# Weighted sums of V move wholly off the matrix engine in eleven of sixteen head groups of a two-layer decode step

## The chip, the cores and the metric

One core of a Trainium2 chip runs the kernel. The metric is the device time of one execution in microseconds (us). The kernel before took 676.72 us (median of 3 runs, 676.02 to 676.72).

## What is computed

A decode step for one token passes twice through an attention block and an MLP block, with the same weights and the same caches both times:

```python
def _A_ref(x, k_cache, v_cache, wq, wo):              # D=512, H=32 heads, Sk=4096 keys, Dh=128
    q = (x @ wq).reshape(B, Sq, H, Dh)                # heads to the front
    scores = jnp.einsum("bhqd,bhkd->bhqk", q, k_cache) * (Dh ** -0.5)
    p = _softmax(scores, axis=-1)
    o = jnp.einsum("bhqk,bhkd->bhqd", p, v_cache)
    return o.reshape(B, Sq, H * Dh) @ wo
def _B_ref(x, w1, b1, w2, b2):                        # F=1376
    return _gelu(x @ w1 + b1) @ w2 + b2
...
x = x + _A_ref(_layernorm(x), ...)
x = x + _B_ref(_layernorm(x), ...)
x = x + _A_ref(_layernorm(x), ...)
x = x + _B_ref(_layernorm(x), ...)
```

All is float32. The caches K and V hold 32 x 4096 x 128 elements each (64 MiB), and each is read once per layer.

## The kernel before, in words

**Groups.** The 32 heads are cut into G = 8 groups of J = 4. A layer runs n = 0 to 7 over the groups (layer 1 in the reverse order of heads, so that it begins with what still lies on the chip). A group's K is 128 x 16384 elements (8 chunks of NC = 2048 columns), its V the same, and one transfer of 128 x 4096 brings two weights: wo for this group and wq for the next.

**What a group does.** `queries` makes the group's queries z: four VectorE (DVE) operations over wq, a TensorE (PE) sum over the partitions, then DVE again. `scores` multiplies z with the 8 chunks of K on PE: 32 matmuls, which the trace shows as 64 passes, into the PSUM tile pS. `softmax` reads pS on DVE, takes the exponential on ScalarE (ACT), transposes on PE, and leaves the weights in pt. Then V is weighted and summed over the keys. `scaled_out` takes this sum from the PSUM tile pO and divides by the softmax's sum, and `head_out` multiplies with wo and adds into one row in the PSUM tile pB.

**Two ways to weight V.** Without `vec` (the groups n = 6 and 7 of layer 0 and all of layer 1), `values` does it on PE: 4 matmuls for each chunk with pt as the small operand. With `vec` (layer 0, n = 0 to 5) six of the eight chunks are multiplied in place, four by DVE (L268) and two by ACT (L265, 32 small operations), DVE adds the six into one chunk (L276, L278), and PE sums this one over its partitions with ones (`add_weighted`, L282) behind the two chunks that it still weights itself (L254). There, `add_weighted`, `scaled_out` and `head_out` of group n are called `late`, after the scores of group n+1 in the program; the program leaves their place on the engines to the framework's scheduler, save for what `pin` and `load` fix in the written order.

**Transfers.** All transfers go through one queue in program order, issued by SyncE (SP, L88). One large SBUF tile, `arena`, is cut by hand into homes. Layer 0 rotates three homes of 8 chunks through K and V. In layer 1, K has one home (columns 8 to 16 NC) and V one (0 to 8 NC). `PAIR` is the single home of the two weights. A transfer waits until all readers of its home are done, and all later transfers wait behind it.

**The end.** In the last group (n = 7, `final`) K comes in two halves and V in pieces, with small matmuls (`idle`, L420) between them; then wo, the MLP's w2 in four pieces, the MLP (`mlp`, its second product at L395), one addition (L598) and the store.

Of the kernel before, what the change touches and what calls it, by code (L numbers as in the profile page):

```python
# [17 lines left out]
P = 128  # L18
# [26 lines left out]
W2_AT = tuple(SPARE + U * (c % 8) for c in range(FB)), tuple(2 * BLOCK + 2 * NC + U * c for c in range(FB))  # L45
# [12 lines left out]
VECTOR, SCALAR = 6, 2  # L58
# [3 lines left out]
def decode_layers(ctx: ExitStack, tc: tile.TileContext, k, v, w, w1, w2, out):  # L62
# [45 lines left out]
    def free_now(layer, n):  # L108

        if layer == 0:  # L110
            at = HELD + 2 * NC
        elif n == 0:
            at = 6 * NC
            return arena[:, at : at + U], arena[:, 11 * NC : 11 * NC + 4 * 129]
        else:
            at = 9 * NC if n == 1 else 2 * BLOCK + NC
# [90 lines left out]
    def queries(n, xc, wt, at, t=None, short=False):  # L207
        t = wt[:, 0, :] if t is None else t
        pin(nc.vector.tensor_scalar(t, wt[:, 0, :], xc[:, 0:1], None, op0=ALU.mult))
        for c in range(1, 4):  # L210
            nc.vector.scalar_tensor_tensor(t, wt[:, c, :], xc[:, c : c + 1], t, op0=ALU.mult, op1=ALU.add)  # L211
        if short:
            nc.tensor.matmul(at, one.to_broadcast([P, P]), t, start=True, stop=True)  # L213
            own = t.rearrange("p (j d) -> p j d", j=J)
            nc.vector.tensor_tensor(own, at.rearrange("p (j d) -> p j d", j=J),
                                    ident[:, None, :].to_broadcast([P, J, P]), op=ALU.mult)
            nc.vector.tensor_reduce(zq[:, :, C - 1], own, axis=AX.X, op=ALU.add)
# [6 lines left out]
    def scores(z, c, kt):  # L224
        for j in range(J):
            nc.tensor.matmul(pS[32 * j : 32 * j + C, :], z[:, j, C - 1 - c : 2 * C - 1 - c],  # L226
                             kt[:, j, :], start=(c == 0), stop=(c == C - 1))

    def softmax(sc, nsc, p):
        nc.vector.tensor_reduce(mx[:, 0:1], pS, axis=AX.X, op=ALU.max)  # L230
# [26 lines left out]
    def weighted(pt, at, a, b):  # L257

        own = arena[:, at + NC * a : at + NC * b].rearrange("p (r j d) -> p r j d", j=J, d=DH)
        for i in range(a, b):  # L260
            t = own[:, 4 * (i - a) : 4 * (i - a + 1)]
            if i >= vec - SCALAR:
                for r in range(4):
                    for j in range(J):
                        nc.scalar.activation(t[:, r, j], t[:, r, j], AF.Copy, scale=pt[:, j, i, r : r + 1])  # L265
                continue
            weight = pt[:, :, i, :].rearrange("p j b -> p b j")[:, :, :, None].to_broadcast([P, 4, J, DH])
            nc.vector.tensor_tensor(t, t, weight, op=ALU.mult)  # L268

    def sum_weighted(at, n):  # L270

        def part_of(a, b):
            return arena[:, at + NC * a : at + NC * b]

        half = n // 2
        nc.vector.tensor_tensor(part_of(0, half), part_of(0, half), part_of(half, n), op=ALU.add)  # L276
        for c in range(1, half):
            nc.vector.tensor_tensor(part_of(0, 1), part_of(0, 1), part_of(c, c + 1), op=ALU.add)  # L278

    def add_weighted(at):  # L280
        for j in range(J):
            nc.tensor.matmul(pO[32 * j : 32 * j + 4, :], one.to_broadcast([P, 4]),  # L282
                             by_head(chunk(arena[:, at : at + NC]))[:, j], start=False, stop=True)
# [22 lines left out]

    def head_out(on, wt, n):
        if layer == 0 and n < G - 1:
            t = wt[:, 0, :]
            nc.vector.tensor_scalar(t, t, on[:, 0:1], None, op0=ALU.mult)  # L310
            for d in range(1, 4):
                nc.vector.scalar_tensor_tensor(t, wt[:, d, :], on[:, d : d + 1], t, op0=ALU.mult, op1=ALU.add)  # L312
            nc.tensor.matmul(pB[0:1, :], one, t, start=n == 0, stop=n == G - 2)  # L313
# [332 lines left out]
```

## Time and profile before

| what | value |
|---|---|
| median of 3 runs | 676.72 us |
| time of the profiled execution | 676.74 us |
| its span, first to last instruction | 674.8 us |
| mean granted TensorE clock | 0.767 of full |
| moved by DMA | 285.31 MB, mean 423 GB/s |
| busy: PE / DVE / ACT | 364.0 / 259.1 / 84.1 us |

A page of the profile lists busy time by engine, a picture of the span in 40 slices, the chain of waits followed back from the last instruction, and groups of instructions by line with the mean duration of one. A timeline gives single instructions with their start from the span's beginning and what ended the idle time before them. PE matmuls in float32 appear as two passes each.

### The profile page before, as it was taken

What the parts mean: (1) busy time and instruction counts of PE and PEld (TensorE: products, weight loads), DVE (VectorE), ACT (ScalarE), POOL (GpSimd) and SP (SyncE); (2) the same over time, 40 slices, a digit from 0 to 9 for tenths busy, and PEclk for the clock granted to TensorE, in tenths of its full rate; (3) what the DMA queues carried; (4) which work ended last, traced back from release to release, by engine and by line L of the source; (5) the groups of instructions that cost most, each with busy time, mean ns of one, the idle gap of its engine ahead of it and who ended that gap; (6) DMA issues with size and microseconds to landing.
All of it is one profiled execution on the core that took longest, in us unless ns stands there. A gap on an engine that the chain in (4) does not pass through costs nothing.

```text
span 674.8 us, 6333 instructions
## 1 busy us (share of the span) xinstructions
PE 364.0 (54%) x2664; PEld 94.1 (14%) x2664; DVE 259.1 (38%) x446; ACT 84.1 (12%) x249; POOL 5.0 (1%) x24
## 2 busy tenths in 40 slices
PE   1521622616426146175887987473355544755596
PEld 1100100101001001011124321111011111111123
DVE  3059379295693964933322322120121011201212
ACT  0041060140500503202011200000000000000010
POOL 1000000000000000000000000000000000000000
PEclk9965766856757668578699999786797677866989
DMA  9999999999999999999999999999999999999995
GB/s 375 435 435 437 435 436 431 418 454 431 432 435 409 455 435 432 435 432 414 428 415 385 404 422 447 421 443 427 435 432 435 436 435 405 451 432 414 431 415 236
DMA packets 10979, 285.31 MB, mean 423 GB/s; under 512 B 1220, under 2 KB 1224, under 8 KB 3400
## 3 DMA queue, kind: packets, MB, share of 16 engines
q1 hardware_dynamic: 10952, 284.92, 98.7%
q8 instruction: 20, 0.33, 0.2%
q14 instruction: 7, 0.06, 0.0%
HBM read 284.92 MB, written 0.00 MB: 422 GB/s over the span
## 4 chain that ended last, share of the span: by engine, by line
DMA 58%; PE 23%; DVE 17%; issue 1%; another core or an unknown queue 0%; ACT 0%; DVEq 0%; SPq 0%; ACTq 0%
DMA arena<-in_k 26%; DMA arena<-in_v 26%; PE pS L226 13%; DMA arena<-in_w 6%; DVE arena L268 5%; DVE arena L276 4%; DVE arena L278 3%; PE pO L254 2%; DVE arena L312 1%; PE pS L420 1%; DVE arena L211 1%; PE pO L282 1%; PE pB L313 1%; PE pB L317 1%; PE pO L395 1%
## 5 line engine op out<-in xcount | busy, mean ns | idle before, releaser
L226 PE MATMUL pS<-arena,smalls 128*8 128x512 f32 x1024 | 148.8, 709 | 57.6 <-DMA arena<-in_k 55.6
L254 PE MATMUL pO<-arena,pt 128*4 128x512 f32 x720 | 107.5, 737 | 55.5 <-DMA arena<-in_v 55.1
L230 DVE TENSOR_REDUCE smalls<-pS 128x1 f32<-128x512 f32 x16 | 11.1, 692 | 199.3 <-PE pS L226 199.3
L236 ACT ACTIVATE arena<-pS,smalls 128x512 f32<-128x512 f32 x16 | 12.4, 777 | 457.1 <-DVE smalls L235 457.1
L213 PE MATMUL pS<-arena,smalls 128*128 128x512 f32 x12 | 12.5, 1141 | 98.6 <-DVE arena L211 98.6
L286 DVE STREAM_TRANSPOSE arena<-pO 128x512 f32<-128x512 f32 x16 | 11.5, 717 | 128.2 <-PE pO L254 124.7
L268 DVE TENSOR_TENSOR arena<-arena,pt 128x2048 f32<-128x2048 f32 x24 | 53.9, 2287 | 15.1 <-DMA arena<-in_v 15.1
L265 ACT ACTIVATE arena<-arena,pt 128x128 f32<-128x128 f32 x192 | 56.7, 386 | 22.0 <-DMA arena<-in_v 22.0
L226 PEld LDWEIGHTS pS<-arena,smalls 128*8 128x8 f32 x1024 | 30.2, 99 | 161.4 <-issue 137.8
L276 DVE TENSOR_TENSOR arena<-arena 128x6144 f32<-128x6144 f32 x6 | 39.3, 6553 | 0.0
L254 PEld LDWEIGHTS pO<-arena,pt 128*4 128x4 f32 x720 | 20.3, 97 | 125.9 <-issue 121.5
L211 DVE SCALAR_TENSOR_TENSOR arena<-arena,smalls 128x512 f32<-128x512 f32 x45 | 33.8, 750 | 0.9
L238 PE MATMUL pO<-ident,arena 128*128 128x128 f32 x64 | 11.4, 305 | 38.0 <-ACT arena L236 37.6
L317 PE MATMUL pB<-arena,smalls 128*1 128x512 f32 x56 | 25.2, 592 | 10.3 <-DVE smalls L291 6.6
L313 PE MATMUL pB<-arena,smalls 128*1 128x512 f32 x14 | 13.1, 1035 | 29.4 <-DVE arena L312 29.4
L278 DVE TENSOR_TENSOR arena<-arena 128x2048 f32<-128x2048 f32 x12 | 27.4, 2288 | 0.0
L213 PEld LDWEIGHTS pS<-arena,smalls 128*128 128x128 f32 x12 | 3.0, 311 | 108.9 <-DVE arena L211 108.9
L312 DVE SCALAR_TENSOR_TENSOR arena<-arena,smalls 128x512 f32<-128x512 f32 x21 | 15.8, 752 | 0.7
L238 PEld LDWEIGHTS pO<-ident,arena 128*128 128x128 f32 x64 | 7.3, 150 | 51.9 <-ACT arena L236 46.5
L420 PE MATMUL pS<-arena,ident 128*8 128x512 f32 (+1 forms) x34 | 14.2, 517 | 0.5 <-DVE pt L354 0.5
L420 PE MATMUL pO<-arena,ident 128*8 128x512 f32 (+1 forms) x30 | 11.6, 507 | 0.3 <-DVE smalls L189 0.3
L282 PE MATMUL pO<-arena,smalls 128*4 128x512 f32 x48 | 11.0, 1006 | 0.8
(114 smaller groups left out, 164.7 us busy)
## 6 DMA issues: line engine op xcount, KB each, us to landing
arena<-in_w SPq DMA_DIRECT2D x14, 2048.0 KB, 22.4
arena<-in_k SPq DMA_DIRECT2D x6, 4096.0 KB, 27.6
arena<-in_v SPq DMA_DIRECT2D x2, 4096.0 KB, 35.4
arena<-in_k SPq DMA_DIRECT2D x3, 2048.0 KB, 13.6
arena<-in_v SPq DMA_DIRECT2D x2, 2048.0 KB, 38.5
arena<-in_w SPq DMA_DIRECT2D x4, 1024.0 KB, 15.0
arena<-in_v SPq DMA_DIRECT2D x3, 1024.0 KB, 46.7
arena<-in_w SPq DMA_DIRECT2D x6, 512.0 KB, 12.2
```

The lines of the kernel that those rows point to most:

```text
L211: nc.vector.scalar_tensor_tensor(t, wt[:, c, :], xc[:, c : c + 1], t, op0=ALU.mult, op1=ALU.add)
L226: nc.tensor.matmul(pS[32 * j : 32 * j + C, :], z[:, j, C - 1 - c : 2 * C - 1 - c], kt[:, j, :], start=(c == 0), stop=(c == C - 1))
L238: nc.tensor.transpose(pT[:, b].rearrange("p j r -> p (j r)"), p[:, P * b : P * (b + 1)], ident)
L254: nc.tensor.matmul(pO[32 * j : 32 * j + 4, :], pt[:, j, c, :], by_head(vt)[:, j], start=(i == 0), stop=(i == of - 1))
L265: nc.scalar.activation(t[:, r, j], t[:, r, j], AF.Copy, scale=pt[:, j, i, r : r + 1])
L268: nc.vector.tensor_tensor(t, t, weight, op=ALU.mult)
L276: nc.vector.tensor_tensor(part_of(0, half), part_of(0, half), part_of(half, n), op=ALU.add)
L278: nc.vector.tensor_tensor(part_of(0, 1), part_of(0, 1), part_of(c, c + 1), op=ALU.add)
L312: nc.vector.scalar_tensor_tensor(t, wt[:, d, :], on[:, d : d + 1], t, op0=ALU.mult, op1=ALU.add)
L313: nc.tensor.matmul(pB[0:1, :], one, t, start=n == 0, stop=n == G - 2)
L317: nc.tensor.matmul(pB[0:1, :], on[:, d : d + 1], wt[:, d, :], start=n == 0 and d == 0, stop=n == G - 2 and d == 3)
L420: pin(nc.tensor.matmul(at[:C, :n], ident[:, :C], t[:, 0, :n], start=True, stop=True))
```

## The change

1. **Layer 0, n = 0 to 5.** All eight chunks of V are weighted off PE: chunks 0 to 3 by DVE (`weighted`), 4 to 7 by ACT (`weighted_by_act`, 64 operations in place of 32). DVE adds in pairs of chunks (`add_pair`, 128 x 4096 elements), three times, and then the last two chunks together.
2. **Layer 1, n = 2 to 6.** The same way is taken where before PE weighted all chunks. In n = 6, the last but one group, PE weights one pair (chunks 2 and 3), DVE four chunks and ACT two. The order of the pairs is given by `PAIRS`.
3. **Place of the late work.** `late` is now two parts. `late_sum` (ones products on PE, `scaled_out`, and wo's four DVE operations into `ot`, a home of its own) stands after chunk 4 of the next group's scores, and after chunk 3 in the final group; `late_out` (one PE product into pB) stands after the scores. These and their neighbours are pinned to the written order.
4. **wo by DVE in layer 1, too.** For n = 1 to 6 of layer 1 `head_out`'s four products on PE become four DVE operations and one product; the queries take the short way there as well. For n = 6 the copy of pB and `row_to_quadrants` come with `late_out`, in the midst of the final group.
5. **Homes.** In layer 1, from n = 2, V alternates between 0 to 8 NC and 6 to 14 NC, K lies from 15 NC (from n = 3) and the softmax's tiles at 14 NC. W2's second home and `ends` move to the low columns.

The core of the diff:

```diff
+        def add_pair(at, to, by):
+            a, b = (arena[:, at + NC * c : at + NC * (c + 2)] for c in (to, by))
+            pin(nc.vector.tensor_tensor(a, a, b, op=ALU.add))
+        def sum_over_keys(t, start):
+            for j in range(J):
+                pin(nc.tensor.matmul(pO[32 * j : 32 * j + 4, :], one.to_broadcast([P, 4]), by_head(t)[:, j],
+                                     start=start, stop=True))
...
             for c, t in tiles:
                 scores(z, c, t)
+                if late is not None and c == (3 if final else 4):
+                    late[0]()
             if late is not None:
-                late()
+                late[1]()
                 late = None
...
-            if vec:
-                weighted(pt, v_home, vec - SCALAR, vec)
-                weighted(pt, v_home, 0, 2)
+            if pairs:
+                first_pair = pairs[0]
+                last = layer == 1 and n == G - 2
+                for c in pairs[2 : 3 if last else 4]:
+                    for i in (0, 1):
+                        weighted_by_act(pt, here["v", g, c + i], c + i)
+                for c in pairs[:2]:
+                    for i in (0, 1):
+                        weighted(pt, here["v", g, c + i], c + i)
+                add_pair(v_home, *pairs[:2])
...
+            if pairs:
+                z = queries(n + 1, xc_l, wq_next, pS, short=True,
+                            between=lambda: add_pair(v_home, first_pair, pairs[2]))
+                if not last:
+                    add_pair(v_home, first_pair, pairs[3])
+                total, other = here["v", g, first_pair], here["v", g, first_pair + 1]
+                pin(nc.vector.tensor_tensor(total, total, other, op=ALU.add))
+                def late_sum(rl=rl, ot=ot, wt=wo_t, total=total, last=last):
+                    sum_over_keys(total, not last)
+                    summed_wo(scaled_out(rl, ot), wt, ot[:, :U])
+                def late_out(ot=ot, n=n):
+                    add_out(ot[:, :U], n)
+                    if n == G - 2:
+                        row = arena[:, PAIR : PAIR + U]
+                        nc.vector.tensor_copy(row, pB)
+                        row_to_quadrants(row)
```

**PE in a group of layer 0.** Before, from one group's softmax transposes (L238) to the next group's (L254: its own two chunks of V; L213: queries; L282: ones; L313: wo's row; L226: scores):

```order
L238 MATMUL pO<-ident,arena 128x128 x4
L254 MATMUL pO<-arena,pt 4x512 x8
L213 MATMUL pS<-arena,smalls 128x512
L282 MATMUL pO<-arena,smalls 4x512 x4
L313 MATMUL pB<-arena,smalls 1x512
L226 MATMUL pS<-arena,smalls 8x512 x32
```

Of the change, the same stretch (scores are L228, ones L277, wo's row L309):

```order
L240 MATMUL pO<-ident,arena 128x128 x4
L213 MATMUL pS<-arena,smalls 128x512
L228 MATMUL pS<-arena,smalls 8x512 x20
L277 MATMUL pO<-arena,smalls 4x512 x4
L228 MATMUL pS<-arena,smalls 8x512 x12
L309 MATMUL pB<-arena,smalls 1x512
```

The eight matmuls over V are gone, and the ones and wo's row no longer stand ahead of the scores.

**DVE in the same group**, from the weighting of V to the queries' last step. Before (L268 weighting, L276 and L278 sums, L209 to L217 queries):

```order
L268 TENSOR_TENSOR arena<-arena,pt 128x2048 x3
L209 TENSOR_SCALAR arena<-arena,smalls 128x512
L268 TENSOR_TENSOR arena<-arena,pt 128x2048
L211 SCALAR_TENSOR_TENSOR arena<-arena,smalls 128x512
L276 TENSOR_TENSOR arena<-arena 128x6144
L211 SCALAR_TENSOR_TENSOR arena<-arena,smalls 128x512
L278 TENSOR_TENSOR arena<-arena 128x2048
L211 SCALAR_TENSOR_TENSOR arena<-arena,smalls 128x512
L278 TENSOR_TENSOR arena<-arena 128x2048
L215 TENSOR_TENSOR arena<-pS,ident 128x512
L217 TENSOR_REDUCE smalls<-arena 128x4
```

Of the change (L273 is `add_pair`, L217 and L219 the queries' last two steps, L557 the sum's last addition):

```order
L268 TENSOR_TENSOR arena<-arena,pt 128x2048 x4
L273 TENSOR_TENSOR arena<-arena 128x4096
L209 TENSOR_SCALAR arena<-arena,smalls 128x512
L211 SCALAR_TENSOR_TENSOR arena<-arena,smalls 128x512 x3
L273 TENSOR_TENSOR arena<-arena 128x4096
L217 TENSOR_TENSOR arena<-pS,ident 128x512
L219 TENSOR_REDUCE smalls<-arena 128x4
L273 TENSOR_TENSOR arena<-arena 128x4096
L557 TENSOR_TENSOR arena<-arena 128x2048
```

Two pair additions now stand ahead of the queries' end, and the rest of the sum behind it. In layer 1 the groups n = 2 to 6 have this same list (n = 6 with one L273 less at the end).

**PE from the last but one group into the final one.** Before (L254 values, L317 wo's four products, L220 queries, L326 the row to its quadrants, L226 the final scores, L420 small matmuls):

```order
L254 MATMUL pO<-arena,pt 4x512 x32
L317 MATMUL pB<-arena,smalls 1x512 x4
L220 MATMUL pO<-smalls,arena 128x1 x4
L326 MATMUL pB<-arena,ident 1x128 x4
L226 MATMUL pS<-arena,smalls 8x512 x32
L420 MATMUL pO<-arena,ident 8x512 x3
L238 MATMUL pO<-ident,arena 128x128 x4
```

Of the change:

```order
L256 MATMUL pO<-arena,pt 4x512 x8
L213 MATMUL pS<-arena,smalls 128x512
L228 MATMUL pS<-arena,smalls 8x512 x16
L277 MATMUL pO<-arena,smalls 4x512 x4
L228 MATMUL pS<-arena,smalls 8x512 x16
L309 MATMUL pB<-arena,smalls 1x512
L326 MATMUL pB<-arena,ident 1x128 x4
L420 MATMUL pO<-arena,ident 8x512 x3
L240 MATMUL pO<-ident,arena 128x128 x4
```

The ones products, wo's row and its quadrants now stand between the final scores and the softmax's transposes. On DVE, the copy of pB stands ahead of the softmax's first reduction there:

```order
L303 TENSOR_SCALAR arena<-arena,smalls 128x512
L305 SCALAR_TENSOR_TENSOR arena<-arena,smalls 128x512 x3
L567 COPY arena<-pB 128x512
L232 TENSOR_REDUCE smalls<-pS 128x1
L234 STREAM_TRANSPOSE smalls<-smalls 128x32
```

Before, that copy (L562) stood ahead of the final scores and their reduction (L230) behind them with nothing of group n = 6 between.

More of the change, by code (lines that the diff above doesn't have):

```diff
@@ L304, in scaled_out_last, with summed_wo, add_out @@
         return on
-    def head_out(on, wt, n):
[L308 to L313, printed above, removed]
+    def summed_wo(on, wt, t):
+        pin(nc.vector.tensor_scalar(t, wt[:, 0, :], on[:, 0:1], None, op0=ALU.mult))
+        for d in range(1, 4):
+            pin(nc.vector.scalar_tensor_tensor(t, wt[:, d, :], on[:, d : d + 1], t, op0=ALU.mult, op1=ALU.add))
+        return t
+    def add_out(t, n):
+        pin(nc.tensor.matmul(pB[0:1, :], one, t, start=n == 0, stop=n == G - 2))
+    def head_out(on, wt, n):
+        if n < G - 1 and (layer == 0 or n > 0):
+            add_out(summed_wo(on, wt, wt[:, 0, :]), n)
             return
@@ L573, in decode_layers @@
         else:
[L575 removed]
+            ends = arena[:, 5 * NC : 5 * NC + 3 * P]
             xb = of_32(ends, 4)
```

90 lines of the change are left out of this document (38 added, 52 removed).

## The prediction

> **What bounds the kernel now.** I read the page first: busy time, the slices, then the chain of waits.
>
> ```profile
> PE 364.0 (54%) x2664; PEld 94.1 (14%) x2664; DVE 259.1 (38%) x446; ACT 84.1 (12%) x249; POOL 5.0 (1%) x24
> DMA  9999999999999999999999999999999999999995
> DMA 58%; PE 23%; DVE 17%; issue 1%; another core or an unknown queue 0%; ACT 0%; DVEq 0%; SPq 0%; ACTq 0%
> ```
>
> No engine is busy for more than 54%, and the transfers never pause until the last slice. The bytes stay as they are. So the change can move the time in two ways only: it lets the queue run dry, or it changes what stands behind the last transfers. First, the queue. The timeline of one group in layer 0, DVE and SP:
>
> ```profile
> 89.62 6.70 DVE L268 TENSOR_TENSOR arena<-arena,pt 128x2048 f32<-128x2048 f32 x3 [3.27 <-DMA arena<-in_v]
> 99.49 6.55 DVE L276 TENSOR_TENSOR arena<-arena 128x6144 f32<-128x6144 f32 x1
> 113.78 0.72 DVE L286 STREAM_TRANSPOSE arena<-pO 128x512 f32<-128x512 f32 x1 [0.63 <-PE pO L282]
> 115.54 2.33 DVE L312 SCALAR_TENSOR_TENSOR arena<-arena,smalls 128x512 f32<-128x512 f32 x3
> 119.81 0.33 SPq L88 DMA_DIRECT2D arena<-in_w  x1
> 127.35 0.69 DVE L230 TENSOR_REDUCE smalls<-pS 128x1 f32<-128x512 f32 x1 [9.48 <-PE pS L226]
> 133.25 2.29 DVE L268 TENSOR_TENSOR arena<-arena,pt 128x2048 f32<-128x2048 f32 x1 [2.11 <-DMA arena<-in_v]
> ```
>
> V lands at 89.6 and the next V at 133.25: 43.6 us for 18 units of 1 MiB (w 2, K 8, V 8), 433 GB/s. The next weights are issued at 119.81, 13.4 us before the transfer ahead of them is in. The queue has that much in reserve. Layer 1, where PE weights V alone, keeps the same pace by the chain, from one K's landing to the next:
>
> ```profile
> 518.65 34.55 DMA arena<-in_k
> 562.64 34.18 DMA arena<-in_k
> ```
>
> They end at 553.20 and 596.82, again 43.6 us apart. Layer 0's DVE and ACT work costs the transfers nothing, and PE's work in layer 1 neither: what is freed there was not waited for.
>
> Now the end, from the chain and PE's timeline:
>
> ```profile
> 606.64 33.89 DMA arena<-in_k
> 640.57 6.61 PE pS L226 x32
> 665.26 0.46 PE pS L343 x16
> 668.78 1.89 issue
> 670.67 1.10 PE pO L395 x32
> ```
>
> From the last half of K (640.53) on, the chain is compute: PE and DVE one behind the other, 28.3 us to 668.78. Then PE stands still for 1.89 us for nothing that the chain can name. The end is thus PE's and DVE's path, and the transfers are some 1 to 2 us ahead of it.
>
> **The change part by part.** *The queue in layer 0 and from n = 2 in layer 1.* I count from V's landing. Four weightings take 4 x 2.23 (6.70 / 3) = 8.9 us. A pair addition of 4096 elements stands between two rows: 6.55 us above and the 2.20 us of L278 below, so 4.4. The queries and their last steps:
>
> ```profile
> 106.71 2.20 DVE arena L278
> 625.96 0.48 DVE L209 TENSOR_SCALAR arena<-arena,smalls 128x512 f32<-128x512 f32 x1
> 626.48 2.33 DVE L211 SCALAR_TENSOR_TENSOR arena<-arena,smalls 128x512 f32<-128x512 f32 x3
> 111.74 0.69 DVE L215 TENSOR_TENSOR arena<-pS,ident 128x512 f32<-128x512 f32 x1
> 112.47 0.69 DVE L217 TENSOR_REDUCE smalls<-arena 128x4 f32<-128x512 f32 x1
> L265 ACT ACTIVATE arena<-arena,pt 128x128 f32<-128x128 f32 x192 | 56.7, 386 | 22.0 <-DMA arena<-in_v 22.0
> ```
>
> 2.85 and 1.42 us. Queries are ready at 8.9 + 4.4 + 2.85 + 4.4 + 1.4 = 22.0 us, the whole sum 4.4 + 2.2 later, at 28.5. ACT's 64 operations take 64 x 56.7 / 192 = 18.9 us, and the last pair is wanted at 22.0: hidden by 3 us. K lands 10 units after V, at 24.2. So queries wait for K, not K for queries. Twenty matmuls of scores come to 30.8 (their pace is below), the ones to about 32, then DVE's 4.1 us (113.78 to 117.87): the weights' home is free at about 36.3, not 30.2 as before (119.81 - 89.62). The reserve falls from 13.4 to 7.3 us but stays. SP's next two issues, K and V, stand behind it and come with it. The softmax begins at 36.3 (before: 127.35, so 37.7) and ends some 4 us later, ahead of V at 43.6. In layer 1 the terms are the same. Its next V waits for the first pair addition only, 13.3 us after V, and K is under way until 24.2: 10.9 us in reserve. All of this is off the path: nothing saved, nothing lost. Without the reserve each late microsecond would count eleven times.
>
> *n = 1 of layer 1.* Four DVE operations in place of PE's products add about 3 us ahead of the queries, which puts the scores of n = 2 at 424 instead of 421.26. The V that they are to weight lands at 440.7: covered.
>
> ```profile
> 421.26 7.05 PE L226 MATMUL pS<-arena,smalls 128*8 128x512 f32 x64 [0.26 <-DVE smalls L221]
> 440.72 9.22 PE L254 MATMUL pO<-arena,pt 128*4 128x512 f32 x64 [8.96 <-DMA arena<-in_v]
> ```
>
> *The final group.* Here K's first half came early, and before the queries were ready just in time for it:
>
> ```profile
> 616.30 8.48 PE L254 MATMUL pO<-arena,pt 128*4 128x512 f32 x64 [5.86 <-DMA arena<-in_v]
> 630.94 3.62 PE L226 MATMUL pS<-arena,smalls 128*8 128x512 f32 x32
> 640.57 6.56 PE L226 MATMUL pS<-arena,smalls 128*8 128x512 f32 x32 [6.01 <-DMA arena<-in_k]
> 629.74 0.69 DVE L562 COPY arena<-pB 128x512 f32<-128x512 f32 x1 [0.94 <-PE pB L317]
> 630.62 0.40 PE L326 MATMUL pB<-arena,ident 128*1 128x128 f32 x8
> 646.96 2.74 PE L420 MATMUL pO<-arena,ident 128*8 128x512 f32 x6
> 649.87 0.66 PE L238 MATMUL pO<-ident,arena 128*128 128x128 f32 x4 [0.18 <-ACT arena L236]
> ...
> 111.83 1.93 PE pO L282 x8
> 466.00 8.54 PE L226 MATMUL pS<-arena,smalls 128*8 128x512 f32 x64 [10.16 <-DMA arena<-in_k]
> 495.78 3.59 PE L317 MATMUL pB<-arena,smalls 128*1 128x512 f32 x8 [1.32 <-DVE smalls L291]
> 647.21 0.69 DVE L230 TENSOR_REDUCE smalls<-pS 128x1 f32<-128x512 f32 x1 [16.32 <-PE pS L226]
> 596.96 9.61 PE L226 MATMUL pS<-arena,smalls 128*8 128x512 f32 x64 [8.56 <-DMA arena<-in_k]
> ```
>
> V of n = 6 is there at 616.3. By the count above the final queries come at 616.3 + 22.0 = 638.3, where before the scores began at 630.94. The two halves of the scores then run one behind the other. The same 32 passes took 3.62 us at full clock and 6.56 after an idle stretch at half clock. PE will have idled, but the clock rises on the way: 64 passes in layer 1 took 8.54 to 9.61 us, so 1.3 to 2.4 us over twice 3.62. I take 5.7 for the first half (bounds 3.6 and 6.6): 644.0. The ones are 8 passes: 1.93 us in layer 0 (L282, at half clock), 0.9 at the scores' full-clock pace; PE has by then worked for 5.7 us, so I take 0.9: 644.9. Then two strands. PE runs the second half, 3.6 us. DVE runs transposes and wo's sum, 4.1 us, to 649.0. DVE is the later. L309 is one matmul, two passes. By the row of L317, eight passes in 3.59 us, it takes 0.9: 649.9. The copy of pB, 0.73 us with its wait: 650.65. Only now does the softmax's reduction start, which before began at 647.21. PE does L326, 0.4, and the three small matmuls, 2.6 (2.74 less the tail of the last): 653.7. DVE and ACT would be ready at 650.65 + 2.66 (647.21 to 649.87) = 653.3. So the transposes begin at 653.7 to 653.9 instead of 649.87: **3.9 us late**, bounds 1.8 (PE warm throughout) and 4.8 to 5.8 (cold throughout, the ones at 1.9).
>
> On the clock the Trainium skill ("TensorE: Matmul & The Clock Gate", Part 1) says that about 3.4 us of sustained work bring the full rate, in free-running windows. By it the first half would take an estimated 5.1 us and the total would be 0.6 us lower; the rows agree in kind (1.3 to 2.4 us lost at 0.092 us a pass is half clock for 2.9 to 5.3 us), and their middle is my 5.7.
>
> Behind the transposes the chain has no wait for data, so the 3.9 us travel down to 668.78. There the 1.89 us of standstill come in.
>
> ```profile
> 668.78:670.67 1.89, 0.00 (x0) 0.00 (x0) 0.00 (x0) 0.00 (x0) 0.00 (x0) 1.00 0.05 17
> q8 instruction: 20, 0.33, 0.2%
> q8 instruction: 1, 0.02, 2.7%
> ```
>
> The data were nearly in (DMA busy 5%), and the second row of instruction fetches is that of 667.5 to 670: one of the page's twenty lies just there. PE has 2664 weight loads and as many matmuls, 266 for each fetch of 16 KB: I read the standstill as PE waiting for code. The change takes 216 float32 matmuls off PE (864 such records, 3.4 fetches), so the boundary moves 0.4 of a fetch along and no longer stands here. It falls some 110 passes before the end, about 5 us of work after the boundary ahead of it. That is nearly the time from one boundary (128 passes earlier, in L343 at about 665.3) to the arrival here at 670.67, so I leave 0.2 us.
>
> The Trainium skill ("Runtime: NRT & Kernel Launch", Instruction fetch mechanics) has fetches of 256 instructions, mostly hidden. The size agrees with the twenty fetches; "hidden" does not agree with the 1.89 us. Were it right and the wait another one, 3.9 us of lateness would swallow that wait just as well: 0.2 us less.
>
> *Sum* against the profiled execution (676.74 us, span 674.8): +3.9 late, -1.89 standstill, +0.2 left = **+2.2 us: 678.9 us**. The median of the runs shown, 676.72, is the same time.
>
> **The rivals.** *The standstill's room takes it in* (no change). If PE is warm in the first half, or the adds or ones are a little shorter, the transposes come 1.8 us late: 676.74 + 1.8 - 1.89 + 0.2 = 676.8. For it: clock windows of all kinds occur here (7.05 us for 64 passes in one group). Against: PE has only one matmul in the 10 us or more ahead of the final scores.
>
> *The standstill comes back*: the new boundary costs what the old one did, in the MLP instead: 676.74 + 3.9 = 680.6. For it, the short margin above.
>
> *The queue runs dry.* If the late strand of a group is longer than 43.6 us from V to V, every such group pays. It decides from 7.3 us over my count; 1 us beyond that is 11 us in all, 688. Against: every term but the 4096-wide addition has its row.
>
> *Faster*, by one mechanism, the pair additions: two of them stand on the final queries' path. Should a 4096-wide one take 2.2 us like a 2048-wide, the queries are there at 633.9, the first half is over before K's second half lands, that half runs warm from 640.6, and the transposes begin at about 649.4: 0.4 us early. The standstill goes: 676.74 - 0.4 - 1.9 = 674.4, or some 675 where the last data bound it. It decides from about 2.6 us for an addition. Against it: 6.55 and 2.20 us for 6144 and 2048 elements are the same 1.07 ns for each.
>
> **How the numbers follow.** My forecast 0.50, no change 0.32, standstill back 0.06, queue dry 0.04, faster 0.08. A measurement here tells about 0.2% (1.35 us) from no change. Slower: 0.50 + 0.06 + 0.04 = 0.60; same 0.32; faster 0.08. The forecast's own range goes from 678.1 to 680.4. With no change taken in, and the standstill back, it is 675.9 to 681.4; the dry queue and most of faster lie outside.
>
> **What would show it.** Steps right: V to V still 43.6 us in both layers; weights issued 6 to 9 us before the transfer ahead lands; the final scores beginning at 638 and the transposes near 653.8; no standstill before the last matmuls. Wrong: an addition (L273) far from 4.4 us, a DMA slice below 9 in the middle, transposes before 652, or a PE standstill between 663 and the end.

## The result: slower by 0.56%, in two places

The changed kernel took 680.45 us (median of 6, 679.99 to 681.44), the kernel before, in the same comparison, 676.54 us (median of 6): a ratio of 1.0056 [1.0046, 1.0067]. In a second comparison it was 680.65 against 677.09 us, again 1.0056 [1.0044, 1.0069]. That is 3.6 to 3.9 us slower; forecast were 2.2 us (678.9) in a range from 675.9 to 681.4.

The profiled execution took 680.01 us, its span 678.2 us, 3.4 more than before. From its page (busy time; the slices of the transfers; the chain of waits):

```profile
PE 299.0 (44%) x2232; PEld 79.2 (12%) x2232; DVE 427.1 (63%) x521; ACT 224.8 (33%) x729; POOL 5.0 (1%) x24
DMA  9999999999999999999999999999999999999994
DMA 21%; DVE 12%; PE 6%; issue 0%; SPq 0%; DVEq 0%
```

PE gave up 65 us, DVE took on 168 us and ACT 141 us, and the transfers still have no pause that a slice of 17 us would show. A group of layer 0, timeline of DVE and of SP:

```profile
89.51 8.90 DVE L268 TENSOR_TENSOR arena<-arena,pt 128x2048 f32<-128x2048 f32 x4 [4.22 <-DMA arena<-in_v]
98.44 4.42 DVE L273 TENSOR_TENSOR arena<-arena 128x4096 f32<-128x4096 f32 x1
...
126.01 0.33 SPq L88 DMA_DIRECT2D arena<-in_w  x1
...
133.12 8.90 DVE L268 TENSOR_TENSOR arena<-arena,pt 128x2048 f32<-128x2048 f32 x4 [3.49 <-DMA arena<-in_v]
```

From V to V it is still 43.6 us. The next weights are issued 7.1 us before the transfer ahead of them is in (13.4 before). All that DVE and ACT do more there costs nothing.

The end, timeline of DVE and PE:

```profile
617.47 8.90 DVE L268 TENSOR_TENSOR arena<-arena,pt 128x2048 f32<-128x2048 f32 x4 [3.33 <-DMA arena<-in_v]
639.29 6.35 PE L228 MATMUL pS<-arena,smalls 128*8 128x512 f32 x32 [3.58 <-DVE smalls L219]
645.47 1.03 PE L277 MATMUL pO<-arena,smalls 128*4 128x512 f32 x8
646.33 3.61 PE L228 MATMUL pS<-arena,smalls 128*8 128x512 f32 x32
646.58 0.72 DVE L281 STREAM_TRANSPOSE arena<-pO 128x512 f32<-128x512 f32 x1 [5.14 <-PE pO L277]
650.72 1.02 PE L309 MATMUL pB<-arena,smalls 128*1 128x512 f32 x2 [0.78 <-DVE arena L305]
651.77 0.69 DVE L567 COPY arena<-pB 128x512 f32<-128x512 f32 x1 [1.11 <-PE pB L309]
652.38 0.68 DVE L232 TENSOR_REDUCE smalls<-pS 128x1 f32<-128x512 f32 x1
655.40 0.66 PE L240 MATMUL pO<-ident,arena 128*128 128x128 f32 x4
672.54 2.58 PE L395 MATMUL pO<-arena,smalls 128*1 128x128 f32 x88
```

V of n = 6 lands at 617.5 (I count from PE's first pass over it, 617.51) and the softmax's transposes begin at 655.40; before, these were 616.30 and 649.87. The last product (L395) now runs in one piece, without the standstill. So the 3.4 us of the span are these: V of n = 6 comes **1.2 us later**, the transposes come 37.89 us after it instead of 33.57 (**4.32 later**), the standstill of 1.89 is gone, and 0.24 are won on the way. From V of n = 6 to the store it is 58.00 us, before 55.81: 2.19 more. The lateness at the end was forecast; the 1.2 us by which the stream of transfers lags were not.

Where the stream lags shows at the start of layer 1. In its first group (n = 0) K and V are still on the chip, and K of n = 2 goes where V of n = 0 lies, so its issue waits until PE has weighted that V. Timeline of DVE and SP in the change:

```profile
382.15 0.17 DVE L223 COPY smalls<-pO 128x4 f32<-128x4 f32 x1 [6.92 <-PE pO L222]
382.22 0.68 DVE L232 TENSOR_REDUCE smalls<-pS 128x1 f32<-128x512 f32 x1
...
394.52 6.14 SPq L88 DMA_DIRECT2D arena<-in_k  x2
```

and in the kernel before:

```profile
378.50 0.69 DVE L230 TENSOR_REDUCE smalls<-pS 128x1 f32<-128x512 f32 x1 [3.41 <-PE pS L226]
...
390.85 0.83 SPq L88 DMA_DIRECT2D arena<-in_k  x2
```

The softmax's reduction, now pinned, stands behind the copy of the queries for n = 1 (L223), which waits for PE. Before, the scheduler had put it ahead (378.50; the copy, there L221, came at 382.00). K of n = 2 is issued at 394.52 instead of 390.85, 2.6 us before the transfer ahead of it lands (397.15), where there were 5.5. The change's windows of 2 us there (the last two columns are the transfers' busy share and GB/s):

```profile
394.00:396.00 2.00, 0.67 (x9) 0.09 (x2) 1.13 (x3) 0.00 (x0) 0.00 (x0) 1.00 1.08 338
396.00:398.00 2.00, 2.00 (x6) 0.41 (x5) 0.00 (x0) 0.00 (x0) 0.00 (x0) 1.00 0.76 317
398.00:400.00 2.00, 2.00 (x18) 0.41 (x17) 0.00 (x0) 0.00 (x0) 0.00 (x0) 1.00 0.89 377
```

Against the 433 GB/s of the steady stream, 95, 116 and 56 GB/s are missing: (95 + 116 + 56) x 2 / 433 = 1.2 us. That this is also the 1.2 us of V of n = 6 is chance. V of n = 1 had landed 0.80 us later than before already (397.15 against 396.35), from there to V of n = 2 it took 0.84 more, and K of n = 3 then came in 19.36 us instead of 20.39. One pair of profiles does not give the price of the late issue; the experiments do.

### The profile page after: what moved, and what is told of

It is laid out like the page before. It is cut to its first block, busy times and chain, and to the rows that moved or that the text cites. A ratio compares the mean times of both kernels' runs of the same rounds, so it can differ in the third digit from the quotient of the medians.

```text
span 678.2 us, 6042 instructions
## 1 busy us (share of the span) xinstructions
PE 299.0 (44%) x2232; PEld 79.2 (12%) x2232; DVE 427.1 (63%) x521; ACT 224.8 (33%) x729; POOL 5.0 (1%) x24
## 5 line engine op out<-in xcount | busy, mean ns | idle before, releaser
L263 ACT ACTIVATE arena<-arena,pt 128x128 f32<-128x128 f32 x672 | 197.5, 387 | 53.3 <-DMA arena<-in_v 51.8
L228 PE MATMUL pS<-arena,smalls 128*8 128x512 f32 x1024 | 148.4, 733 | 81.7 <-DMA arena<-in_k 74.8
L273 DVE TENSOR_TENSOR arena<-arena 128x4096 f32<-128x4096 f32 x32 | 141.4, 4420 | 0.4
L268 DVE TENSOR_TENSOR arena<-arena,pt 128x2048 f32<-128x2048 f32 x44 | 97.9, 2286 | 38.9 <-DMA arena<-in_v 38.6
L213 PE MATMUL pS<-arena,smalls 128*128 128x512 f32 x22 | 22.8, 1141 | 213.9 <-DVE arena L211 213.9
L238 ACT ACTIVATE arena<-pS,smalls 128x512 f32<-128x512 f32 x16 | 12.4, 778 | 287.0 <-DVE smalls L237 256.0
L228 PEld LDWEIGHTS pS<-arena,smalls 128*8 128x8 f32 x1024 | 30.0, 103 | 203.8 <-issue 179.4
L256 PE MATMUL pO<-arena,pt 128*4 128x512 f32 x320 | 47.6, 688 | 8.9 <-DMA arena<-in_v 8.1
L211 DVE SCALAR_TENSOR_TENSOR arena<-arena,smalls 128x512 f32<-128x512 f32 x45 | 33.8, 752 | 1.6
L213 PEld LDWEIGHTS pS<-arena,smalls 128*128 128x128 f32 x22 | 5.5, 311 | 218.9 <-DVE arena L211 218.9
L305 DVE SCALAR_TENSOR_TENSOR arena<-arena,smalls 128x512 f32<-128x512 f32 x39 | 29.3, 752 | 1.4
L309 PE MATMUL pB<-arena,smalls 128*1 128x512 f32 x26 | 14.7, 651 | 25.5 <-DVE arena L305 25.5
L557 DVE TENSOR_TENSOR arena<-arena 128x2048 f32<-128x2048 f32 x11 | 25.2, 2292 | 0.3
L244 DVE STREAM_TRANSPOSE smalls<-smalls 128x32 f32<-128x32 f32 x16 | 3.4, 212 | 17.5 <-ACT arena L238 17.5
L420 PE MATMUL pS<-arena,ident 128*8 128x512 f32 (+1 forms) x34 | 14.2, 517 | 0.5 <-DVE pt L354 0.5
L256 PEld LDWEIGHTS pO<-arena,pt 128*4 128x4 f32 x320 | 8.8, 93 | 39.3 <-issue 37.9
## 6 DMA issues: line engine op xcount, KB each, us to landing
arena<-in_v SPq DMA_DIRECT2D x3, 1024.0 KB, 46.6
```

What stands on the lines that cost most here:

```text
L211: pin(nc.vector.scalar_tensor_tensor(t, wt[:, c, :], xc[:, c : c + 1], t, op0=ALU.mult, op1=ALU.add))
L213: pin(nc.tensor.matmul(at, one.to_broadcast([P, P]), t, start=True, stop=True))
L228: pin(nc.tensor.matmul(pS[32 * j : 32 * j + C, :], z[:, j, C - 1 - c : 2 * C - 1 - c], kt[:, j, :], start=(c == 0), stop=(c == C - 1)))
L256: nc.tensor.matmul(pO[32 * j : 32 * j + 4, :], pt[:, j, c, :], by_head(vt)[:, j], start=(i == 0), stop=(i == of - 1))
L263: nc.scalar.activation(own, own, AF.Copy, scale=pt[:, j, c, b : b + 1])
L268: nc.vector.tensor_tensor(own, own, weight, op=ALU.mult)
```

## The experiments

Two theories. **The late end**: the loss is the chain behind V of n = 6. **The stream**: the loss is that the transfers run late, at the start of layer 1 or in all middle groups. All times are compared with runs of the kernel before on the same chip, and the profile of each gives three more numbers: from V of n = 1 to V of n = 2 landing in layer 1 (the stream at the start of the layer), from V of n = 6 to the transposes and to the store (the end). The change was timed in two comparisons with one ratio, the other kernels beside it or on other chips; where two ratios are subtracted below, the difference is uncertain by about 0.15%, 1 us (both intervals taken together).

| kernel | ratio to before, 95% | V to V | V to transposes | V to store |
|---|---|---|---|---|
| before | 1 | 44.23 | 33.57 | 55.81 |
| the change | 1.0056 [1.0046, 1.0067] | 45.07 | 37.89 | 58.00 |
| the change, in a second comparison | 1.0056 [1.0044, 1.0069] | 45.71 | 38.01 | 58.12 |
| n = 6 of layer 1 back on PE | 1.0016 [1.0005, 1.0028] | 46.58 | 31.81 | 54.68 |
| lighter end | 1.0024 [1.0013, 1.0034] | 45.72 | 35.10 | 55.50 |
| first softmax of layer 1 free | 1.0020 [1.0011, 1.0029] | 43.81 | 37.05 | 57.16 |
| both: n = 6 on PE, softmax free | 0.9986 [0.9977, 0.9994] | 43.81 | 31.60 | 55.12 |
| the same, on another chip | 0.9984 [0.9976, 0.9993] | 44.91 | 31.67 | 54.23 |
| only layer 0 changed | 1.0010 [1.0001, 1.0019] | 45.49 | 31.95 | 55.76 |
| before, code moved by 160 | 1.0005 [0.9995, 1.0015] | 44.21 | 32.03 | 55.34 |
| queries first | 1.0054 [1.0040, 1.0067] | 47.12 | 37.85 | 57.97 |
| fillers ahead of the first half | 1.0114 [1.0100, 1.0129] | 47.10 | 41.58 | 61.69 |
| queries first, with fillers | 1.0152 [1.0139, 1.0165] | 44.76 | 43.67 | 63.79 |
| all kept off PE, with fillers | 1.0080 [1.0064, 1.0097] | 43.81 | 40.69 | 60.81 |

**1. n = 6 of layer 1 back on PE.**

```diff
-            if layer == 1 and 1 < n < G - 1:
+            if layer == 1 and 1 < n < G - 2:
```

With it the copy of pB and the quadrants stand ahead of the final scores again. 

> The changed kernel with the last but one group of layer 1 (n = 6) put back: PE weights its V, and its sum, wo's row and the row's quadrants stand ahead of the final scores again; the other ten groups stay changed. Tail theory (the loss is the final group's late queries and the late work in the midst of its scores): the final transposes come at about 651 instead of 655.4, but 80 more PE instructions put a code boundary 55 to 60 instructions before the end again, so a standstill of some 1.7 us is back: 677.7 us, 2.7 less than the changed kernel. Queue theory (each changed group lets the transfers fall behind): ten of eleven groups are still changed, so 680.0 or more.

Measured: 678.41 us against 677.13, 1.0016 [1.0005, 1.0028]. Some 0.40% of the 0.56%, 2.7 us, are back. Its timeline on PE:

```profile
618.78 9.04 PE L256 MATMUL pO<-arena,pt 128*4 128x512 f32 x64 [4.73 <-DMA arena<-in_v]
638.36 9.48 PE L228 MATMUL pS<-arena,smalls 128*8 128x512 f32 x64 [0.97 <-DVE smalls L219]
650.59 0.66 PE L240 MATMUL pO<-ident,arena 128*128 128x128 f32 x4 [0.18 <-ACT arena L238]
670.86 2.22 PE L395 MATMUL pO<-arena,smalls 128*1 128x128 f32 x56 [0.17 <-DMA arena<-in_w]
```

The transposes begin 31.8 us after V and the last product waits for weights again, not for the chain ahead of it. The late end is a cause, but not the whole: V of n = 6 landed at 618.8, 2.5 us later than before. The standstill of 1.7 us that the expectation had back did not come: the chain has 0.06 us of "issue" there.

**2. A lighter end.** The row in pB is copied by ACT instead of DVE, and three small matmuls (`idle`) ahead of the softmax's transposes are left out in the final group of layer 1; they compute nothing that is used.

```diff
-                        nc.vector.tensor_copy(row, pB)
+                        nc.scalar.copy(row, pB)
...
-                for _ in range(FILL if final or layer == 1 else 0):
+                for _ in range(FILL if layer == 1 and first or final and layer == 0 else 0):
```

> The changed kernel, but in the final group of layer 1 the row is copied out of pB by ScalarE in place of VectorE, and the three small matmuls between the scores and the transposes are left out. Tail theory: VectorE's reduction no longer waits for the copy (it starts at about 650.8 in place of 652.4) and PE is free at 653; transposes at 653.4 in place of 655.4, so 2.0 us less: 678.4 us. Queue theory: no change, 680.4.

Measured: 678.74 us, 1.0024 [1.0013, 1.0034], 0.32% or 2.2 us less than the change. Timeline on PE:

```profile
652.36 0.40 PE L326 MATMUL pB<-arena,ident 128*1 128x128 f32 x8 [0.67 <-ACT arena L567]
653.18 0.66 PE L240 MATMUL pO<-ident,arena 128*128 128x128 f32 x4 [0.42 <-ACT arena L238]
```

The transposes come 0.8 us behind the quadrants (L326) instead of 2.9. Another 0.6 us of the 2.79 by which the transposes come sooner after V is the first half of the scores, which took 5.72 us here (6.35 in the change) without being touched by these edits. What is taken off this chain comes off the time: it is the bound.

**3. The first softmax of layer 1 free.**

```diff
-        pin(nc.vector.tensor_reduce(mx[:, 0:1], pS, axis=AX.X, op=ALU.max))
+        (pin if layer == 0 or not first else id)(nc.vector.tensor_reduce(mx[:, 0:1], pS, axis=AX.X, op=ALU.max))
```

> The changed kernel, but the first reduction of the softmax is not pinned in the first group of layer 1, so that VectorE does it ahead of the copy of the next group's queries, as in the kernel before. Theory that the 1.2 us by which the last transfers come later than before (V of n = 6 at 617.4, was 616.3) is lost where K of n = 2 is issued only 2.6 us ahead of need (394.52, was 390.85): K is issued at about 391.5 again, V of n = 6 lands at 616.3 and the time falls by about 1.1 us to 679.3. Rival (the transfers' own unevenness, code fetches among them, which the order of layer 1's first group does not touch): K is issued earlier, but V of n = 6 still lands near 617.4 and the time stays at 680.4.

Measured: 678.73 us, 1.0020 [1.0011, 1.0029]. 0.36% or 2.4 us are back, twice the 1.1 expected. Its timeline, DVE and SP:

```profile
379.91 0.69 DVE L232 TENSOR_REDUCE smalls<-pS 128x1 f32<-128x512 f32 x1 [3.41 <-PE pS L228]
...
391.86 6.14 SPq L88 DMA_DIRECT2D arena<-in_k  x2
```

and its windows:

```profile
396.00:398.00 2.00, 2.00 (x24) 0.50 (x17) 0.00 (x0) 0.00 (x0) 0.00 (x0) 1.00 1.19 512
398.00:400.00 2.00, 2.00 (x27) 0.43 (x22) 0.00 (x0) 0.00 (x0) 0.00 (x0) 1.00 0.95 410
```

K is issued 5.9 us ahead of need and the rate stays up. V of n = 6, though, landed at 617.10, not at the 616.3 expected: V of n = 1 was 0.7 us later here than in the change (397.81), so the gain shows from V to V (1.26 us) and not in the landing. The price of the pin was more than the 1.2 us of one profile: the eight profiles with the pin take 45.9 us from V to V in the mean (44.8 to 47.1), the six without it 44.1 (43.8 to 44.9), 1.8 us apart. In the pinned ones the issue came 0.8 to 3.0 us ahead of need, without the pin 5.5 to 7.0. The two pinned ones with 0.8 us took 46.6 and 47.1 us; a third with 47.1 had 2.2 us and lost 1.6 in a later transfer. The 0.6 us between 1.8 and 2.4 lie within the uncertainty. In this profile the end is 0.84 us shorter, too, because the first half of the final scores took 5.50 us in place of 6.35; no run shows that the pin has a part in that.

**4. Both undone.** Edits 1 and 3 together, timed on two chips; as in edit 1, the copy of pB and the quadrants stand ahead of the final scores.

```diff
-        pin(nc.vector.tensor_reduce(mx[:, 0:1], pS, axis=AX.X, op=ALU.max))
+        (pin if layer == 0 or not first else id)(nc.vector.tensor_reduce(mx[:, 0:1], pS, axis=AX.X, op=ALU.max))
...
-            if layer == 1 and 1 < n < G - 1:
+            if layer == 1 and 1 < n < G - 2:
```

> n = 6 of layer 1 back on PE, and the softmax of layer 1's first group free to begin when it could before. n = 6 alone left 0.16% (1.1 us) over the kernel before. Theory that this rest is layer 1's first group, whose softmax waits for the queries' copy and so delays an issue by some 3 us: ratio 1.0000 (0.9990 to 1.0008). Rival, that the rest is in the middle groups (layer 0 and n = 2 to 5), where the weights and V are issued with less in reserve: 1.0016 again.

> The kernel with both parts undone once more, beside the others: if it is truly faster than the kernel before, 0.9977 to 0.9994 again; if the first 0.9986 was chance, 1.0000.

Measured: 676.03 against 677.09 us, 0.9986 [0.9977, 0.9994]; again 676.11 against 676.93, 0.9984 [0.9976, 0.9993]. It is not the 1.0000 expected but faster than the kernel before, by about 1 us. The two edits give back 0.40, 0.36 and together 0.70%, so the whole loss is in these two places, and a little more than the loss. The chain of its last 50 us, then its transposes:

```profile
625.24 29.50 DMA arena<-in_v
654.75 12.65 DMA arena<-in_w
667.53 1.04 PE pO L395 x29
668.57 1.04 issue
669.61 1.05 PE pO L395 x27
```

```profile
635.34 9.41 PE L228 MATMUL pS<-arena,smalls 128*8 128x512 f32 x64 [0.97 <-DVE smalls L219]
647.49 0.66 PE L240 MATMUL pO<-ident,arena 128*128 128x128 f32 x4 [0.18 <-ACT arena L238]
```

The transposes stand 31.6 us after V, 2.0 earlier than in the profile of before. The final scores do not begin earlier: wo of n = 6 is summed by DVE now, and the scores begin 19.45 us after V (before: 14.64). But K's second half lands (640.1) before the first is through, so all 64 passes run in one piece of 9.41 us. Before, PE stood still for 6.01 us between the halves, and the second took 6.56 us at half clock. These 2 us do not explain the gain of about 1 us, since the end is set by transfers here: in the kernel before with its code moved (experiment 6) the transposes stand 32.03 us after V, too, and the time stays. What makes this kernel faster than before is not shown.

**5. Layer 0 alone.**

```diff
-            if layer == 1 and 1 < n < G - 1:
+            if False:
```

> The change in layer 0 only (in layer 1 PE weights all chunks again; wo there is still summed by DVE, and the first group's softmax is pinned as in the change). If the rest of 0.16% that n = 6 alone left is the first group's softmax: 1.0016 again. If it is the work of n = 2 to 5 in layer 1: 1.000. If it is layer 0's smaller reserve: 1.0016 as well, and the kernel with both undone tells these two apart. A loss of the whole change in layer 0's queue would show as 1.004 or more.

Measured: 677.61 us, 1.0010 [1.0001, 1.0019]. Here, too, the copy of pB and the quadrants stand ahead of the final scores, and the first softmax is pinned (45.49 us from V to V). Beside the 1.0016 of edit 1 this leaves n = 2 to 5 of layer 1 no price that these intervals show; nor has layer 0 one, since both undone, which has all ten of these groups off PE, is faster than before. Both undone, timed beside it, took 676.03 us, 1.6 less than this kernel, near the 1.8 us of the pin from V to V.

**6. The standstill.** In the kernel before, 40 tiny matmuls at the start of layer 0, which compute nothing used, shift PE's code by 160 instructions (loads, passes):

```diff
+        if layer == 0:
+            for _ in range(40):
+                pin(nc.tensor.matmul(pK[0][:C, :8], ident[:, :C], ident[:, :8], start=True, stop=True))
```

> The kernel before with 40 tiny matmuls (8 columns of the identity, into a PSUM tile not yet in use) at the start, where PE waits for the first K: 160 more PE instructions shift every code boundary, the last from some 64 instructions before the end to some 224. Theory that the 1.89 us standstill at 668.78 is PE waiting for code: it goes, and the time falls by about 1.7 us to 674.9 (the last product is then bound by the last w2 piece). Rival (PE waits there for the last transfer): the standstill and the time stay, 676.5.

Measured: 677.16 us against 677.13, 1.0005 [0.9995, 1.0015]: no gain. Its chain ends so:

```profile
624.41 34.62 DMA arena<-in_v
659.04 11.41 DMA arena<-in_w
670.59 1.01 PE pO L395 x24
```

and the timeline on PE has the second half of the final scores:

```profile
640.94 4.94 PE L226 MATMUL pS<-arena,smalls 128*8 128x512 f32 x32 [5.97 <-DMA arena<-in_k]
```

The standstill is not there. The last part of the last product begins when weights have landed (670.45), and the last of them landed at 671.11, 1.4 us later than in the profile of before. The transfers end at about the time at which the standstill ended, so taking it away gave nothing. Whether it was a wait for code stays open: in the kernel with both undone the same 1.04 us of "issue" stand before the same part of L395, but there the last weights landed at 669.31, within it, and the second profile of that kernel has no such gap. The second half of the scores took 4.94 us here and 6.56 in the profile of before, on the same order of work: the granted clock was half from 640.2 to 643.7 here, from 639.7 to 646.5 there. So the 33.57 us from V to the transposes of before are one execution's, and 32.03 another's.

**7. The queries first.** In n = 6 of layer 1 both pair additions go behind the final queries.

```diff
-                add_pair(v_home, *pairs[:2])
+                if not last:
+                    add_pair(v_home, *pairs[:2])
...
-                            between=lambda: add_pair(v_home, first_pair, pairs[2]))
-                if not last:
+                            between=None if last else lambda: add_pair(v_home, first_pair, pairs[2]))
+                if last:
+                    add_pair(v_home, *pairs[:2])
+                    add_pair(v_home, first_pair, pairs[2])
+                else:
                     add_pair(v_home, first_pair, pairs[3])
```

> In n = 6 of layer 1 the two pair additions (2 x 4.42 us) come behind the final queries. Theory of the late end: the queries are ready some 6.5 us sooner (about V + 15.3), the first half of the scores is over before K's second half lands, and what is then late is the sum of V, ready at about 643.7: ones to 644.6, wo's DVE operations to 648.7 instead of 650.67. So the transposes come 2.0 us sooner than in the change and the time is 2.0 us (0.30%) less. Rival, the stream: what came late is the last transfers, and the ratio stays that of the change, within 0.05%.

> The change itself, beside the three kernels that each undo a part of it, so that all are held against the same runs of the kernel before. If its loss is its own (the end's lateness), the ratio is again 1.0046 to 1.0067, some 3 to 4.5 us. If a part of the first figure came from the chip it ran on, the ratio falls to the 1.002 of the runs with parts undone, and what those parts seemed to give back was nothing.

Measured beside each other: 681.02 and 680.65 us, 1.0054 [1.0040, 1.0067] and 1.0056 [1.0044, 1.0069]. No gain, though not for the reason of the rival. V landed at 621.2 in this execution; timeline on PE, then the window of the second half (the third number from the end is the granted clock):

```profile
636.52 6.52 PE L228 MATMUL pS<-arena,smalls 128*8 128x512 f32 x32 [1.50 <-DVE smalls L219]
647.71 1.89 PE L277 MATMUL pO<-arena,smalls 128*4 128x512 f32 x8 [4.67 <-DVE arena L561]
649.37 5.24 PE L228 MATMUL pS<-arena,smalls 128*8 128x512 f32 x32
```

```profile
647.00:655.00 8.00, 7.29 (x42) 1.36 (x42) 4.52 (x8) 0.00 (x0) 0.00 (x0) 0.65 0.96 410
```

Queries (V + 15.2) and sum (V + 26.4) came as worked out. But PE now waits 4.7 us for the sum, its clock falls, and the ones take 1.89 us where they took 1.03, the second half 5.24 where it took 3.61. The row is in pB at the same 34.2 us after V. The gain went into the clock.

**8. Fillers for the clock.** Matmuls of 512 columns into an unused PSUM tile (`idle(wo_t, pK[0])`), which compute nothing used: ten between the final queries' product and the first half; or three there and fourteen ahead of the ones, with the queries first; or the latter with edits 2 and 3.

```diff
+                for _ in range(10 if last else 0):
+                    idle(wo_t, pK[0])
                 total, other = here["v", g, first_pair], here["v", g, first_pair + 1]
...
+                    for _ in range(14 if last else 0):
+                        idle(wt, pK[0])
                     sum_over_keys(total, not last)
```

> The change with ten matmuls of 512 columns into an unused PSUM tile, on PE between the final queries' product and the first half of the final scores, where PE otherwise idles for 3.6 us. If the half clock after the idle stretch makes the 6.35 us of that half, it now takes 3.6 to 4.0, everything behind it comes 2.4 to 2.7 us sooner (transposes about 652.8 where V of n = 6 lands at 617.5), and the ratio falls by 0.35 to 0.4% to 1.0018 (1.0005 to 1.0030). Rival, that the half waits for something else (its K, or a bank): the half still takes over 5.5 us and the ratio stays above 1.0045.

> The order of the kernel with the queries first, and fillers on PE: three ahead of the first half, fourteen between it and the ones. Theory that the clock ate the 2.0 us expected there (ones 1.89 instead of 0.9, second half 5.24 instead of 3.6): the ones take about 1.0, the second half 3.6, wo's row ends near V + 32.4 instead of V + 34.2, and the time is 1.8 to 2.0 us (0.28%) under the change's: 1.0028 (1.0015 to 1.0040). Rival, that this order costs by itself: 1.0045 or more again.

> All groups of the change kept off PE, with what cost it mended: the first softmax of layer 1 free, queries of n = 6 ahead of the pair additions with the fillers, the row copied by ACT, and the three small matmuls behind the final scores left out. By the terms: softmax's reduction near V + 31.5 (before: V + 30.9), the last weights at V + 53.4 bound the end, and the time is that of the kernel with both parts undone, 0.9986 (0.9975 to 1.0000). Rival, that the way off PE in n = 6 costs by itself: 1.0010 or more.

Measured: 684.81, 687.33 and 681.81 us against 676.93, 1.0114 [1.0100, 1.0129], 1.0152 [1.0139, 1.0165] and 1.0080 [1.0064, 1.0097]. All three are far slower than either theory had it, by my sizing of the fillers. Timeline on PE of the ten:

```profile
637.87 9.81 PE L420 MATMUL pK<-arena,ident 128*8 128x512 f32 x19
...
647.52 3.59 PE L228 MATMUL pS<-arena,smalls 128*8 128x512 f32 x28
```

I had given a filler's pass the 0.2 us of the scores' passes at half clock. It takes 0.5. The ten end at 647.5, about 6 us after the scores could have begun. The fourteen take 11.75 us for 27 passes, so these times say nothing of the order of the work, and the kernel with all groups off PE and its faults mended was not settled. The windows of this profile do answer the question on the clock:

```profile
637.00:640.00 3.00, 3.00 (x5) 0.38 (x4) 3.00 (x1) 0.00 (x0) 0.00 (x0) 0.50 0.91 393
640.00:643.00 3.00, 3.00 (x7) 0.59 (x6) 2.96 (x4) 0.00 (x0) 0.00 (x0) 0.85 1.12 481
643.00:647.00 4.00, 4.00 (x10) 0.81 (x9) 0.66 (x1) 0.00 (x0) 0.00 (x0) 1.00 0.93 401
```

Half clock until about 640.9 (0.85 over 3 us is half for 0.9), 5 us after PE began work at 635.86; then full, and 28 of the first half's 32 passes run in 3.59 us, where the 32 took 6.35. So it is the clock that makes the 6.35 us.

## Why the prediction was right, and where it was off

- **The queue in the groups of pairs**: right. V to V 43.6 us, reserve of the weights 7.1 us (7.3 worked out), a pair addition 4.42 us (4.4), queries 21.8 us after V (22.0).
- **n = 1 of layer 1**: the scores of n = 2 begin at 429.07, estimated 424. 2.4 us of the difference are the pin (426.68 with both undone). Most of the rest is the estimate of 3 us for four DVE operations and a product in place of PE's products: from the first step of this work to the scores it is 4.4 us more (417.44 to 426.68 with both undone, 416.43 to 421.26 before). Covered all the same, V lands at 442.2.
- **The step that failed**: "All of this is off the path: nothing saved, nothing lost" went from n = 2 on and added n = 1, and left out n = 0 of layer 1. The pin on the softmax's reduction acts there too, without any of the moved work; it took 3 of the 5.5 us of reserve at the tightest issue of the layer. The rival "the queue runs dry" was looked for in eleven groups at a microsecond each; it came in a twelfth place, once, at 1.2 us by the rates of one profile, 1.8 us in the mean of the profiles and 2.4 us by the run that frees it.
- **The final group**: right in mechanism, a little small. First half 6.35 us (5.7, bounds 3.6 to 6.6; 5.50, 5.72 and 6.46 in the three other profiles with this order of work up to there), ones 0.9 (0.9), DVE's strand 646.58 to 650.67, 4.1 (4.1), L309 1.02 (0.9). The transposes come 37.89 us after V, worked out were 37.4 to 37.6: 4.3 us late instead of 3.9.
- **The clock**, where the Trainium skill ("TensorE: Matmul & The Clock Gate", Part 1) was weighed against the rows: half clock lasted 5.5 us of the first half here (6.35 less 3.61, twice), 3.8 in the kernel with the first softmax free (5.50 us), and 5 us under the fillers. In the kernel before, the second half spent 5.9 us at half clock (6.56), and 2.6 with its code moved (4.94). The Trainium skill's 3.4 us lie inside these 2.6 to 5.9 us, and its free-running windows agree with the spread. For the first half, the middle of the rows (5.7 us) was nearer than the estimate of 5.1 by the Trainium skill.
- **The standstill**: gone, as forecast, and no new one came. But it is not shown that it was code, and not that it cost the kernel before anything on the whole (experiment 6). For the sum it made no difference: the chain that comes 4.3 us late covers it either way, as the prediction noted. The Trainium skill ("Runtime: NRT & Kernel Launch", Instruction fetch mechanics) has such fetches mostly hidden; the 1.0005 [0.9995, 1.0015] does not speak against it.
- **The sum**: +2.2 for the end, measured 2.19 from V of n = 6 to the store. That the two agree so closely is chance: the lateness was 0.4 us more than worked out, and in place of the 0.2 us left over 0.24 were won. The rest of the 3.4 us between the profiles is the 1.2 us of the stream, which the sum put at nothing. The 680.45 us lie just above the forecast's own 678.1 to 680.4; they lie within the wider range only because that left room for a standstill coming back, which did not come. That it held is luck.
- **The rivals**: the room of the standstill did not take the lateness in. "Faster" stood on a cheap pair addition; it takes 4.42 us. A version near the change is faster than before, the one with both parts undone (0.9986 and 0.9984), though not by this way; by which is not shown.

## What to carry to other kernels

A pin is an edit of its own: it acts in every group that runs through the line, so each group with a tight issue has to be worked through, also those whose work does not change. Where one issue has only some 3 us in reserve, a microsecond on the engine ahead of it is about a microsecond of the stream (1.2 to 1.5 us lost over 43.6 with 2.6 to 3.0 us in reserve, 3.0 to 3.5 with 0.8), and it shows in the end as a later last transfer, not as a wait. And a gap on PE of 3.6 to 6 us cost twice here: the wait, and half clock for 2.6 to 5.9 us after it, so that work brought forward can lose what it won. How long varies from one execution to the next, so a microsecond or two between two profiles of such a chain is not yet an effect.

## What the runs showed of the hardware

- Scores' passes of 512 columns, four in turn into four groups of 32 PSUM partitions, take 3.61 us for 32, 0.113 us each; passes into a single group, like the fillers or L309, take about 0.43 to 0.5 us each (L309: 1.02 us for two; L317 before: 3.59 for eight). By these rows (4 x 0.113 = 0.45) four passes into four groups run at the same time. The Trainium skill ("TensorEngine Tiling (Array Packing)", Overview) has up to four times where a dimension is at most 32 (here the eight columns of z); the rows agree, and the sizing of the fillers overlooked it.
- An issue 2.6 us before the transfer ahead of it landed was too late (1.2 us lost); with 0.8 us some 3 us over the 43.6 were lost, with 5.5 or more 0.2 to 0.6, save one execution that lost 1.3 with 7.0.
- Landings differ between executions by steps of about 1 us at varying places of the stream: V of n = 6 came between 615.9 and 621.3 us, and some of that in single transfers with ample reserve (K of n = 3 in layer 1 took 20.4 us in the kernel before, 19.4 in the one with its code moved).
